# First loads of an attention and token-mixing kernel in another order: half of k by a hardware queue, p by the casting queue, and a new step list

## The chip, the cores and the metric

The kernel runs on one core of a Trainium2 chip. The metric is the device time of one execution in microseconds, median of the runs. A core has five engines, each with an instruction stream of its own that runs in order: TensorE (PE, with its weight loads shown as PEld), VectorE (DVE), ScalarE (ACT), GpSimd (POOL) and SyncE (SP). They wait for each other by semaphores. Transfers go over 16 DMA engines and are issued from SP, ACT or POOL. In this kernel a transfer issued by POOL also casts (float32 in memory, bfloat16 in the buffer); the profile lists POOL's queue as q0, software_dynamic. Transfers issued by SP (q1) and ACT (q10) are hardware_dynamic, and copy without a cast.

## The reference

There are 8 batches of 8 heads, with 576 positions of 64 elements, and 32 packing queries `p` for each head. Attention is applied twice, then a token-mixing layer.

```python
def sm_attn(qq, kk, vv):
    s = scale * np.matmul(qq, kk.transpose(0, 1, 3, 2))
    a = np.exp(s - np.max(s, axis=-1, keepdims=True))
    a = a / (np.sum(a, axis=-1, keepdims=True) + 1e-09)
    return np.matmul(a, vv)
p_packed = sm_attn(p, k, v)                # 32 rows for each head
x = sm_attn(q, p_packed, p_packed)         # then heads side by side: (8, 576, 512)
wq, wk = x @ w_q, x @ w_k                  # 512 -> 64
W_tok = scale * np.einsum('bsd,btd->bst', wq, wk)
mixed = np.einsum('bst,btd->bsd', W_tok, x)
out = np.maximum(mixed, 0.0) @ w_out       # 512 x 512
```

Inputs and output are float32. The output has 9.4 MB, as have q, k and v each.

## The kernel before

The whole program is one string, `ORDER`, at the head of the file. Each item is a step, with the batch and part after dots, the engine after `@` (A is ACT, V is DVE, P is POOL, S is SP), and the banks of the PSUM after `=`. The loop at the end of the kernel goes through the string and issues each step. As every engine runs its own stream in order, the string fixes the order on each engine, and the order of the transfers on each queue; between engines only the data's dependences count. Nothing is left to a scheduler.

The steps of one batch b, in the order of the data:

- `LD.k`, `LD.v` (two transfers), `LD.q` bring in the batch on POOL's casting queue (L156 to L181). There are four buffers each. In batch 0, k and q come in two halves (`LD.h0`, `LD.g0` for k, `LD.r0`, `LD.q0` for q).
- `KT` and `QV` transpose k and q in blocks on DVE (L236, the helper of all such transposes).
- `S1` (L281, TensorE) multiplies p with k; `X1` (L292, ACT) takes the exponential; `TE` (DVE) transposes it; `PV` (L314) multiplies with v and, by a column of ones in v's buffer, sums up; `RC`, `PP` (DVE) divide and mask, `PT` transposes. The result is p_packed.
- `QK` (L335) multiplies p_packed with the small weights w_q and w_k, `QKE` copies it out, `QD` doubles a part of it on POOL.
- `S2` (L372) multiplies q with p_packed in chunks of rows; `X2` (L377, ACT), `RS` (L393), `RR` (L398, DVE) are the softmax's exponential, sum and reciprocal; `AM` (L404, mostly POOL) multiplies; `AT` (L413, L418) transposes the result on TensorE and `AE` copies it out.
- `WKQ` (L440, L445), `WE`, `GM` (L466), `GE`, `Y` (L476), `YE`, `MX` (L491), `MR` (L497), `RL`, `RLR`, `RLF` (L502, L504) are the token mixing with its relu; instead of the 576 x 576 matrix `W_tok` the kernel goes by a small one of 64 columns (`GM`, `Y`), which gives the same product.
- `OT`, `OH` (L539, L576) multiply with w_out, whose load is `LD.O`; `OE`, `OEF`, `OEH` copy out of the PSUM on ACT or DVE (L127, L131); `ST`, `STF`, `STH` store.

Batches overlap: the steps of three or four of them are interleaved by hand in the string. Stores on SP stand behind `HOLD.v7`, a tiny transfer that waits for the last v.

`WARM.n` issues float32 matmuls of n x 128 columns on zeros (L614), with no use for the result: they are fill on TensorE where the string expects it to wait, and run in its stream in order like any other step. `WARM.n.128` issues them 128 columns at a time.

The start of before: p comes in two halves by the hardware queues (`LD.N0` on ACT, `LD.N1` on SP, L160) as float32 into `p32`; `NC` casts them (DVE and ACT), `PX` transposes them into `pT`. The small weights follow on the same queues (`LD.W0`, `LD.W1`, L163) into `w32`; `WC` casts them on POOL. POOL's queue starts with k of batch 0 (`LD.h0`, `LD.g0`), then v, q, and k of batch 1.

All buffers of this start lie in the six output buffers `T["o"]`, which are not yet in use.

Of the kernel before, what the change touches and what calls it, by code (L numbers as in the profile page):

```python
# [647 lines left out]
```

## Time and profile before

| | |
|---|---|
| median of three runs | 104.16 us (104.09 to 104.93) |
| the profiled execution | 104.06 us |
| its span, first to last instruction | 102.2 us |
| TensorE (PE) busy | 92.8 us, 91% |
| DVE busy | 73.5 us |
| ACT busy | 65.1 us |
| POOL busy | 53.3 us |
| granted TensorE clock | 1.0 of full speed |
| transfers | 25.13 MB, casting queue 17.04 MB |

The page's second part shows the span in 40 slices of 2.55 us; a digit is a busy share in tenths. A row of instructions has the start, the duration, the engine, the line of the kernel, the operation, what it writes and reads, and a count if several stand together; in brackets stands how long the engine idled before it and what ended that. A row of a transfer's issue has its size and the time from the issue to the landing. A "landing" is when the data may be used.

### The profile page before, as it was taken

How to read it: one execution, taken by the hardware profiler on the slowest of the kernel's cores; microseconds unless marked ns; L12 is line 12 of the kernel's file. 1: busy time of each engine (PE TensorE's matmuls, PEld its weight loads, DVE VectorE, ACT ScalarE, POOL GpSimd, SP SyncE). 2: the span in 40 equal slices, each digit the busy share in tenths (PEclk: the TensorE clock that was granted, in tenths of full speed). 3: DMA queues.
4: the chain of work that ended last, by engine and by line, in shares of the span. 5: the costliest groups of instructions: out<-in, count | busy, mean ns of one | idle time of the engine just before them, and what ended most of it. 6: DMA issues, size and time to landing. Idle time of an engine off the chain costs nothing.

```text
span 102.2 us, 3594 instructions
## 1 busy us (share of the span) xinstructions
PE 92.8 (91%) x1536; PEld 54.6 (53%) x1536; DVE 73.5 (72%) x140; ACT 65.1 (64%) x111; POOL 53.3 (52%) x83
## 2 busy tenths in 40 slices
PE   5997999998599999999998899989999999999940
PEld 3895445555275633755636556643757564743420
DVE  4273396858978579888697979599999979349510
ACT  1320315198654767849977979887989897726440
POOL 5982877974039929724459483649715009300000
PEclk9999999999999999999999999999999999999999
DMA  1999999999999999999999999999999999997894
GB/s 25 257 233 208 213 211 215 204 213 208 207 208 209 212 208 212 214 208 208 213 208 208 214 211 206 214 210 211 249 249 391 410 418 408 417 389 281 330 368 153
DMA packets 13567, 25.13 MB, mean 246 GB/s; under 512 B 1072, under 2 KB 6448, under 8 KB 13552
## 3 DMA queue, kind: packets, MB, share of 16 engines
q0 software_dynamic: 9936, 17.04, 84.6%
q1 hardware_dynamic: 3056, 7.34, 18.7%
q10 hardware_dynamic: 560, 0.52, 1.9%
q8 instruction: 12, 0.20, 0.7%
q14 instruction: 3, 0.02, 0.1%
HBM read 30.15 MB, written 9.44 MB: 387 GB/s over the span
## 4 chain that ended last, share of the span: by engine, by line
PE 50%; DMA 21%; DVE 8%; POOL 7%; ACT 7%; issue 3%; SPq 1%; POOLq 0%; DVEq 0%; ACTq 0%
PE ps L539 26%; DMA q_sb<-in_q_dram 13%; DMA o<-in_moe_w_q_dram 8%; PE ps L372 4%; POOL a L404 4%; PE ps L314 3%; ACT e1T L292 3%; PE ps L418 3%; PE ps L445 3%; DVE rs L393 2%; PE ps L440 2%; PE ps L466 2%; PE ps L281 2%; ACT e L377 1%; DVE qT L236 1%
## 5 line engine op out<-in xcount | busy, mean ns | idle before, releaser
L539 PE MATMUL ps<-wout,relu 128*128 128x512 bf16 x124 | 30.6, 380 | 0.0
L404 POOL TENSOR_TENSOR a<-e,rr 128x256 bf16<-128x256 f32 (+2 forms) x18 | 19.5, 1098 | 16.9 <-DVE rr L398 6.4
L614 PE MATMUL ps<-o 128*128 128x128 f32 (+3 forms) x76 | 19.3, 398 | 1.2 <-DVE o L134 1.2
L539 PEld LDWEIGHTS <-relu 128*128 128x128 bf16 x124 | 10.7, 98 | 11.7 <-issue 1.1
L127 ACT ACTIVATE o<-ps 128x1024 f32<-128x1024 f32 (+2 forms) x13 | 11.4, 878 | 5.4 <-PE ps L539 5.2
L614 PEld LDWEIGHTS ps<-o 128*128 128x128 f32 x76 | 11.2, 206 | 5.3 <-issue 3.6
L502 ACT ACTIVATE relu<-ps 128x1024 bf16<-128x1024 f32 (+1 forms) x14 | 12.9, 967 | 1.1 <-PE ps L491 1.1
L292 ACT ACTIVATE e1T<-ps 128x576 bf16<-128x576 f32 x16 | 9.8, 655 | 5.3 <-PE ps L281 4.7
L377 ACT ACTIVATE e<-ps 128x256 f32<-128x256 f32 (+2 forms) x19 | 11.2, 622 | 2.8 <-PE ps L372 2.6
L393 DVE TENSOR_REDUCE rs<-e 128x16 f32<-128x512 f32 (+2 forms) x13 | 10.9, 841 | 2.3 <-ACT e L377 2.2
L236 DVE STREAM_TRANSPOSE kT<-k_sb 128x1152 uint32<-128x1152 uint32 (+1 forms) x9 | 11.0, 1226 | 2.0 <-DMA k_sb<-in_k_dram 2.0
L172 POOL DMA_DIRECT2D v_sb<-in_v_dram x16 | 10.0, 629 | 4.6 <-DMA v_sb<-in_v_dram 1.4
L236 DVE STREAM_TRANSPOSE qT<-q_sb 128x1152 uint32<-128x1152 uint32 (+1 forms) x10 | 11.0, 1112 | 0.4 <-DMA q_sb<-in_q_dram 0.2
L131 DVE COPY o<-ps 128x1024 f32<-128x1024 f32 (+2 forms) x7 | 6.6, 958 | 5.0 <-PE ps L539 2.7
L236 DVE STREAM_TRANSPOSE e<-e1T 128x288 uint32<-128x288 uint32 x16 | 7.4, 469 | 2.5 <-ACT e1T L292 2.0
L127 ACT ACTIVATE aT<-ps 128x128 bf16<-128x128 f32 (+2 forms) x11 | 5.0, 465 | 5.7 <-PE ps L418 3.3
L314 PE MATMUL ps<-v_sb,e 64*64 64x192 bf16 x288 | 7.7, 245 | 0.8 <-DVE e L236 0.5
L127 ACT ACTIVATE wkq<-ps 128x448 bf16<-128x448 f32 (+1 forms) x10 | 7.2, 729 | 1.8 <-PE ps L445 1.7
L314 PEld LDWEIGHTS <-e 64*64 64x64 bf16 x288 | 6.0, 107 | 2.7 <-DVE e L236 2.0
L372 PEld LDWEIGHTS <-qT 64*128 64x128 bf16 x320 | 5.4, 94 | 2.8 <-DVE qT L236 1.8
L372 PE MATMUL ps<-ppT,qT 64*128 64x64 bf16 x320 | 6.6, 190 | 0.3 <-DVE qT L236 0.2
L445 PE MATMUL ps<-aT,pqk 128*128 128x256 bf16 (+1 forms) x48 | 6.8, 246 | 0.0
(70 smaller groups left out, 131.7 us busy)
## 6 DMA issues: line engine op xcount, KB each, us to landing
v_sb<-in_v_dram POOLq DMA_DIRECT2D x16, 288.0 KB, 14.3
out_dram<-o SPq DMA_DIRECT2D x9, 512.0 KB, 8.6
k_sb<-in_k_dram POOLq DMA_DIRECT2D x7, 576.0 KB, 13.8
q_sb<-in_q_dram POOLq DMA_DIRECT2D x6, 576.0 KB, 13.5
out_dram<-o POOLq DMA_DIRECT2D x4, 512.0 KB, 9.4
out_dram<-o SPq DMA_DIRECT2D x5, 256.0 KB, 2.6
q_sb<-in_q_dram POOLq DMA_DIRECT2D x4, 288.0 KB, 10.5
out_dram<-orem SPq DMA_DIRECT2D x3, 256.0 KB, 7.7
```

Of the source, the lines that this page charges most:

```text
L127: nc.scalar.activation(o, i, COPY)
L172: nc.gpsimd.dma_start(v_bufs[b % NL][halves(i), 0:7:2], src)
L236: nc.vector.transpose(o, i)
L292: nc.scalar.activation(e1T[:, x], T["s1", b][x].rearrange("a c m -> a m c"), EXP, scale=scale)
L314: nc.tensor.matmul(T["pv", b][halves(cc), i], lhsT, rhs, start=n == 0, stop=n == R - 1, skip_group_check=True)
L372: nc.tensor.matmul(ps[:, y, t - t0, i], lhsT, rhs, start=e == 0, stop=e == 1)
L377: nc.scalar.activation(e2[:, t0:t1].rearrange("a t (i y n) -> a y (t i) n", i=2, y=2), T["s2", b, c].rearrange("a y t i n -> a y (t i) n") ...
L393: nc.vector.tensor_reduce(rs[:, t0 * H:t1 * H], src, axis=AX, op=ADD)
L404: e.tensor_tensor(a2[:, t0:t1].rearrange("a t i (u l) -> a (t i u) l", l=L), e2v(b, c), T["rr", b][:, t0 * H:t1 * H].to_broadcast((P, (t1 ...
L502: nc.scalar.activation(o, i, RELU)
L539: nc.tensor.matmul(ps, lhsT, wout[:, j, :], start=j == 0, stop=j == NJ - 1)
L614: nc.tensor.matmul(bank(int(bk), [w]), warm[:, 0:P], rhs, start=True, stop=True)
```

## The change

Four things change.

- `LD.h0` on the casting queue becomes `LD.H`, the first transfer on SP: the first half of k of batch 0 comes as float32 into `h32` (in output buffer 0). A new step `HC` casts it on ACT. The small weights, both now on SP, stand behind it; their buffer `w32` moves to output buffer 5.
- `LD.N0` and `LD.N1` go to the head of POOL's casting queue and write bfloat16 into `pbf` directly; the step `NC` and the buffer `p32` go. `LD.g0`, v, and q follow.
- On POOL, `LD.k1` stands behind `SET.aff`, `SET.mask`, `SET.v2` and `SET.v3`, and the casts of the small weights behind `LD.k1`. `LD.v2`, `LD.q2`, `LD.O`, `LD.k3` come behind the `AM` steps of batch 0.
- The string is laid out anew, to its end. The steps are the same (but for those named and the fill), in another interleaving, with other PSUM banks, and for some 35 of them another engine (ACT and DVE swap copies; three stores swap POOL and SP).

```diff
 ORDER = """
-LD.N0@A LD.N1@S SET.warm@V SET.v0@V SET.aT0@V SET.aT1@V SET.aT2@V SET.idf@V LD.W0@A LD.W1@S SET.tab@A LD.h0
-LD.g0 LD.v0 LD.r0 LD.q0 LD.k1 NC.0@V PX.0@V NC.1@A PX.1@V SET.aff@P SET.idb@V SET.v3@P KT.0.0@V SET.mask@P
-WC.1@P WC.0@P LD.k2 SET.v1@P LD.v1 SET.v2@P KT.0.1@V WARM.4=0 WARM.22.128=0 S1.0=0,1,2,3 X1.0.1@A TE.0.1@V
-X1.0.0@A TE.0.0@V WARM.8=4 PV.0.0=4,5 PV.0.1 RC.0@V PP.0.0@V PP.0.1@V LD.q1 PT.0@V WARM.6=6 QK.0=6 QKE.0@A
-QV.0.0@V QV.0.1@V QD.0@P WARM.4=7 S2.0.2=2,3 X2.0.2@A RS.0.2@V RR.0.2@V S2.0.0=0,1 LD.v2 S2.0.1=4,5 X2.0.0@A
...
-TE.1.1@V MX.0.0=4,5 X1.2.0@A LD.O PV.1.0=0,1 TE.2.0@V PV.1.1 X1.2.1@A TE.2.1@V RC.1@V LD.k3 PP.1.0@V PP.1.1@V
-PT.1@V MX.0.1=6,7 QV.1.2@V RLR.0@A QK.1=2 QKE.1@V RL.0.0@A WARM.3=3 S2.1.2=4,5 S2.1.0=0,1 RL.0.1@A X2.1.2@A
...
+LD.H@S LD.W0@S LD.W1@S SET.warm@V SET.v0@V SET.aT0@V SET.aT1@V SET.aT2@V SET.idf@V SET.tab@A LD.N0 LD.N1 LD.g0
+LD.v0 LD.r0 LD.q0 SET.aff@P HC@A KT.0.0@V PX.0@V PX.1@V KT.0.1@V SET.idb@V WARM.4=0 WARM.18.128=0 S1.0=0,1,2,3
+X1.0.0@A TE.0.0@V X1.0.1@A TE.0.1@V WARM.9=4 PV.0.0=4,5 SET.mask@P PV.0.1 RC.0@V SET.v2@P SET.v3@P PP.0.1@V
+PP.0.0@V PT.0@V LD.k1 WC.0@P WC.1@P QV.0.0@V WARM.6=6 QK.0=6 QKE.0@A LD.k2 QV.0.1@V WARM.6=7 S2.0.2=0,1
+X2.0.2@A RS.0.2@V SET.v1@P LD.v1 S2.0.1=2,3 S2.0.0=4,5 LD.q1 RR.0.2@V X2.0.1@A RS.0.1@V RR.0.1@V AM.0.2@P
...
+TE.2.1@V PV.1.0=2,3 PV.1.1 RC.1@V LD.v2 MR.0=0,1 RLR.0@A PP.1.0@V PP.1.1@V PT.1@V LD.q2 MX.0.1=4,5 RL.0.1@A
+LD.O MX.0.0=6,7 QK.1=0 QKE.1@A TE.2.0@V RL.0.0@A QV.1.2@V WARM.7=1 S2.1.2=2,3 LD.k3 X2.1.2@A LD.v3 RS.1.2@V
...
+S2.3.3=6,7 MX.2.0=2,3 TE.4.1@V X2.3.3@A OT.1.1 MX.2.1=0,1 RS.3.4@V RL.2.0@A PV.4.0=6,7 PV.4.1 LD.q5 RC.4@V
+RL.2.1@A OT.2.0=2,3 OT.2.1 RR.3.4@V AM.3.3@P OE.1.0@A PP.4.1@V PP.4.0@V OE.2.0@A PT.4@V QK.4=0 AT.3.3=1
...
+X1.6.0@A TE.6.0@V GM.4=6 X1.6.1@A OT.3.2=2,3 HA.5@P LD.r7 GE.4@A Y.4=4,5 QD.5@P OE.3.0@A LD.q7 TE.6.1@V
+PV.6.0=6,7 PV.6.1 RS.5.4@V YE.4@A RR.5.4@V AM.5.3@P MX.4.0=0,1 RC.6@V PP.6.0@V MR.4=4,5 RLR.4@A OT.3.3
...
+RLR.6@A MX.6.1=4,5 OT.5.1 RL.6.1@V AT.7.1=0 RL.6.0@A AM.7.0@P AT.7.0=1 AE.7.0@V OE.5.0@A AE.7.1@V ST.5.0
+OT.6.0=6,7 WKQ.7.0=4,5 WKQ.7.1 WKQ.7.2 WE.7.1@V ST.1.0 OT.6.2=2,3 OEF.6.2@V WE.7.0@A GM.7=1 GE.7@V ST.5.1
...
+OEF.7.0@A STF.7.1 STF.7.0 OEF.7.2@A STF.7.2 OH.7.0=3 OEH.7.0@A STH.7.0 OH.7.1=5 OEH.7.1@A STH.7.1@A
 """
...
-            (nc.sync if eng == "S" else nc.scalar).dma_start(p32[:, i * n:(i + 1) * n], src[i])
+            nc.gpsimd.dma_start(pbf[:, i * n:(i + 1) * n], src[i])
...
-        elif a == "h":
-            nc.gpsimd.dma_start(k_in[0][:, 0], pairs(k, 0)[:, 0])
+        elif a == "H":
+            nc.sync.dma_start(h32, pairs(k, 0)[:, 0])
...
-    p32 = T["o"][NO - 1].rearrange("a t n -> a (t n)")[:, 0:L * Dh // 2]
+    w32 = T["o"][NO - 1][:, 0].rearrange("a (x i n) -> a x i n", x=2, i=2)
+    h32 = T["o"][0].rearrange("a t n -> a (t n)")[:, 0:RQ * Dh]
...
-    w32 = T["o"][0][:, 0].rearrange("a (x i n) -> a x i n", x=2, i=2)
...
-    def NC(x, eng, bk):
-        n = L * Dh // 4
-        copy(eng, pbf[:, x * n:(x + 1) * n], p32[:, x * n:(x + 1) * n])
...
+    def HC(eng, bk):
+        copy(eng, k_in[0][:, 0], h32)
```

The fill of before, in order, is WARM.4, 22 (ahead of `S1.0`), 8 (ahead of `PV.0`), 6 (ahead of `QK.0`), 4 (ahead of `S2.0`), 6, 5, 3 (among the `AT.0`), 2, 3, 1, 5: 75 units of 128 columns. After it is 4, 18, 9, 6, 6, 6, 5, 3, 3, 1, 7 (between `QK.1` and `S2.1`), 4, 4, 1: 77 units. Behind `def NC` the lines of the changed file have numbers smaller by one.

More of the change, by code (lines that the diff above doesn't have):

```diff
@@ new lines @@
+AE.1.2@A AE.1.0@A PT.2@V WARM.1=4 QK.2=4 AT.1.1=5 WKQ.1.0=0,1 QKE.2@A WKQ.1.2 AE.1.1@A WKQ.1.1 WE.1.1@A
+QV.2.2@V S2.2.2=6,7 X2.2.2@A LD.q3 S2.2.3=2,3 WE.1.0@V GM.1=4 GE.1@V LD.v4 OT.0.2=0,1 Y.1=6,7 X2.2.3@A YE.1@A
+OT.0.0=4,5 MR.1=2,3 RLR.1@A MX.1.0=6,7 RL.1.0@A OT.0.3 OE.0.1@A RS.2.4@V RR.2.4@V OT.0.1 QD.2@P AM.2.2@P
+KT.3.2@V S1.3=2,3,6,7 X1.3.0@A OT.1.4=0 AT.2.2=1 OE.0.0@V X1.3.1@A TE.3.0@V TE.3.1@V AM.2.3@P AT.2.3=2
+MX.1.1=4,5 PV.3.0=6,7 AE.2.2@A PV.3.1 AE.2.3@V WKQ.2.0=2,3 WKQ.2.2 WKQ.2.1 OEF.1.4@A RC.3@V PP.3.0@V RL.1.1@A
@@ L589, in STF @@
         q.dma_start(orows(b)[:, :, t * D:(t + 1) * D], T["o", b][:, t])
-    steps = dict(NC=NC, WC=WC, PX=PX, PB=PB, KT=KT, S1=S1, X1=X1, TE=TE, PV=PV, RC=RC, PP=PP,
+    steps = dict(HC=HC, WC=WC, PX=PX, PB=PB, KT=KT, S1=S1, X1=X1, TE=TE, PV=PV, RC=RC, PP=PP,
                  PT=PT, QK=QK, QKE=QKE, QD=QD, QV=QV, S2=S2, X2=X2, HA=HA, RS=RS, RR=RR, AM=AM,
```

60 lines of the change are left out of this document (24 added, 36 removed).

## The prediction

> **What bounds the kernel now.** I read the page's slices first, then TensorE's busy time in three stretches, then the chain of work that ended last, then the landings of the loads beside the instructions that wait for them. The profiled execution took 104.06 us, its span is 102.2, so 1.86 us lie outside the span; the median of the runs is 104.16, 0.10 more. All sums below are made against 104.06.
>
> ```profile
> span 102.2 us, 3594 instructions
> PE   5997999998599999999998899989999999999940
> DMA  1999999999999999999999999999999999997894
> L614 PE MATMUL ps<-o 128*128 128x128 f32 (+3 forms) x76 | 19.3, 398 | 1.2 <-DVE o L134 1.2
> ```
>
> Two rows are nearly full: the DMA engines from the second slice on, and TensorE almost everywhere. But 19.3 us of TensorE's 92.8 are fill, the WARM matmuls of L614: 75 units of 128 columns, 0.257 us each.
>
> ```profile
> 8.68:35.30 26.62, 23.83 (x462) 13.95 (x463) 19.15 (x41) 13.44 (x28) 17.62 (x28) 1.00 1.15 210
> 35.30:98.40 63.10, 61.43 (x1035) 34.33 (x1031) 50.63 (x85) 49.17 (x81) 29.38 (x38) 1.00 1.08 272
> 98.40:102.20 3.80, 0.00 (x0) 0.00 (x0) 0.04 (x1) 0.38 (x1) 0.00 (x0) 1.00 0.63 225
> ```
>
> Each row is a stretch, its length, busy time (and instructions) of TensorE, weight loads, VectorE, ACT and POOL, the granted clock, DMA share and GB/s. From 35.3 us (first product with wout) to 98.4 TensorE idles 63.10 - 61.43 = 1.67 us and has no fill: this stretch is bound by its work, and a new layout can win at most these 1.67 us in it. Before 35.3 TensorE is busy too, but much of that is fill; there it waits for loads, for chains of small steps and, in order, for its own fill. The granted clock is 1.00 everywhere, across an idle of 0.54 us before S1.0 too.
>
> ```profile
> 1.50 7.96 DMA o<-in_moe_w_q_dram
> 9.58 0.54 POOL wqk L129 x2
> 13.64 13.18 DMA q_sb<-in_q_dram
> 26.84 1.39 DVE qT L236
> 28.28 0.31 PE ps L372 x6
> 35.48 0.86 PE ps L539 x4
> ```
>
> The chain of work says the same: POOL waits until 9.5 for the small weights, which holds back its next loads; then q of batch 1 takes 13.18 us from issue to landing (26.82), its transpose starts at once, and S2.1 (28.28) leads by the softmax and the transposes to OT.0 at 35.48. So what counts before 35.3 is when loads land, and which steps are tied to them.
>
> ```profile
> 1.95 0.55 POOL L156 DMA_DIRECT2D k_sb<-in_k_dram  x1
> k_sb<-in_k_dram POOLq DMA_DIRECT2D x1, 288.0 KB, 6.6
> 8.62 0.78 DVE L236 STREAM_TRANSPOSE kT<-k_sb 128x576 uint32<-128x576 uint32 x1 [1.01 <-DMA k_sb<-in_k_dram]
> 9.45 0.47 PE L281 MATMUL ps<-kT,pT 32*32 32x288 bf16 x30 [0.54 <-DVE kT L236]
> 2.49 1.26 POOL L172 DMA_DIRECT2D v_sb<-in_v_dram  x2
> v_sb<-in_v_dram POOLq DMA_DIRECT2D x1, 288.0 KB, 8.6
> 11.78 0.94 PE L314 MATMUL ps<-v_sb,e 64*64 64x192 bf16 x36
> 14.48 1.13 PE L614 MATMUL ps<-o 128*128 128x512 f32 x2
> 15.54 0.78 PE L372 MATMUL ps<-ppT,qT 64*128 64x64 bf16 x40
> ```
>
> The second half of k lands at 1.95 + 6.6 = 8.55 and its transpose waited for it; S1.0 follows at 9.45. The second of the two v loads, issued half-way through the pair at 3.12, lands at 3.12 + 8.6 = 11.7, and PV.0 starts at 11.78. So the start is tied to the queue of loads.
>
> **The change, part by part.** (a) The loads. Bytes read are the same before and after, in another order and by other queues.
>
> ```profile
> o<-in_p_dram ACTq DMA_DIRECT2D x1, 256.0 KB, 3.7
> o<-in_moe_w_q_dram SPq DMA_DIRECT2D x1, 128.0 KB, 8.0
> q10 hardware_dynamic: 36, 0.07, 94.7%
> q1 hardware_dynamic: 13, 0.03, 34.0%
> q0 software_dynamic: 15, 0.03, 45.0%
> q10 hardware_dynamic: 118, 0.06, 43.8%
> q1 hardware_dynamic: 22, 0.01, 10.3%
> ```
>
> The first three queue rows (packets, MB, share) are the first packets of each queue: ACT's at 2.2 to 2.6 us, SP's at 3.0 to 3.4, the casting queue's at 3.8 to 4.2. The last two are weights, at 5.5 to 6.0 and at 8.5 to 9.0, their end. SP's p was issued at 0.74 as ACT's was; I take its 0.8 us delay for its standing behind ACT's. H now stands alone on SP, so it should move from 2.2. Its 590 KB take 1.45 us at the stores' 410 GB/s and 2.3 us at 257 GB/s (page, second slice); I take 1.6, since the casting queue is silent until 3.8. ACT's p had its last packets at about 3.6 and landed at 0.74 + 3.7 = 4.44, so a landing takes some 0.85 us: H lands at 4.7 (bounds 4.5 to 6.2, the latter with SP's old start).
>
> Casting queue: before, two halves of k (590 KB written) passed from 3.8 to 7.7; at the steady 210 GB/s they need 2.8, so 1.1 us were lost to p's rest (some 0.14 MB) and the weights (0.26 MB). Now p (262 KB written) and half of k (295 KB) need 2.65; only the weights disturb, 1.1 x 0.26/0.40 = 0.7. The half of k lands at 3.8 + 2.65 + 0.7 + 0.9 = 8.05, 0.5 us sooner. Bounds: nothing lost to the weights, 7.35; H with SP's old start, half of it still to move at 3.8, 0.9 later, 8.95. As the queue is served in order and never empties, v, q and k1 to wout shift alike: -0.5, ends -1.2 and +0.4.
>
> POOL's issues: k1 now stands behind the affine select, the mask and two memsets of v (0.32 + 0.18 + 0.78 + 0.61 + 0.61, the last two kinds by the rows below), so at about 8.1 instead of 5.02; q0 still moves until about 13.5, so this is hidden. The weights' casts come after k1 instead of ahead of it; k2, v1, q1 behind them as before. v2, q2 and wout go behind AM.0 (to about 20.3 instead of 15.5): q1's packets run until 25.9, so hidden; cover 4 us.
>
> ```profile
> 6.05 0.61 POOL L205 MEMSET v_sb<- 128x576 uint32 x1
> 6.80 0.78 POOL L212 MEMSET mask<- 32x64 bf16 x4
> 5.61 0.63 ACT L127 ACTIVATE o<-o 128x512 bf16<-128x512 f32 x1 [2.05 <-DMA o<-in_p_dram]
> 6.27 0.64 DVE L236 STREAM_TRANSPOSE pT<-o 128x256 uint32<-128x256 uint32 x1 [0.67 <-ACT o L127]
> ```
>
> (b) Casts. The two casts of p go (0.46 DVE, 0.63 ACT); HC, 128x1152 on ACT, is new: at most 2.25 x 0.63 = 1.4, I take 1.2. VectorE: H 4.7 + 1.2, KT.0.0 0.73, PX 2 x 0.64 gives 7.9, before the half of k lands. Ready, no cost.
>
> (c) S1.0 to S2.0. Transpose at 8.05, S1.0 at 8.9 (was 9.45). The fill ahead of it has 22 units instead of 26 and ends sooner; an idle of 1 to 2 us. Behind S1.0 (0.4) nine units instead of eight, 9 x 0.25 = 2.25: PV.0 at 11.55, though v lands at 11.2 (was 11.78: -0.2). From PV.0 to S2.0 it was 15.54 - 11.78 = 3.76 with ten units; now twelve, 4.26: S2.0 at 15.8 (+0.25), though q lands at 14.1. The fill gives the loads' gain away.
>
> (d) S2.0 to OT.0.
>
> ```profile
> 26.41 0.31 DVE L236 STREAM_TRANSPOSE ppT<-pp 128x128 uint32<-128x128 uint32 x1
> ```
>
> AM.0 on POOL keeps its length. On VectorE TE.2.0 (0.47) now stands between PT.1 and QV.1. PT.1 ended at 26.41 + 0.31 = 26.72; PV.1 loses MR.0 and MX.0.0 ahead of it but inherits the +0.25, so PT.1 ends near 26.5, QV.1 starts at 27.0, not at q1's landing of 26.3, and ends at 28.4. TensorE has seven units (1.75) behind QK.1 at 26.8: 28.55. S2.1 at 28.5 (+0.25). From there 7.2 us to OT.0 as before; nine units instead of six (+0.75) fill a wait of about 0.7. OT.0: +0.3, ends -0.5 (all fill fits) and +1.2 (loads late, below).
>
> (e) 35.3 to 98.4. The same matmuls. Its larger waits:
>
> ```profile
> 54.29 0.62 PE L418 MATMUL ps<-idb,a 128*128 128x128 bf16 x8 [0.44 <-POOL a L404]
> 57.05 0.48 PE L281 MATMUL ps<-kT,pT 32*32 32x288 bf16 x32 [0.32 <-DVE kT L236]
> 67.97 0.94 PE L314 MATMUL ps<-v_sb,e 64*64 64x192 bf16 x36 [0.47 <-DVE e L236]
> ```
>
> The last goes: OT.3.2 (0.86) now runs ahead of PV.6 while VectorE makes TE.6; next late would be AT.5.3, whose AM.5.3 ends with it. The first grows by 0.15, as RC.4 now stands ahead of RR.3.4; the second stays (AE.3.3, KT.5 as before). -0.3, ends -1.67 (all idle gone) and +1.2 (as many new waits of 0.3 to 0.5 as these three). The 30-odd evictions that swap between ACT and VectorE cost nothing there: ACT idles 14 us and VectorE 12 of 63; without that cover each costs its 0.3 to 1.0 us. Of the loads, v7 goes behind AM.4 on POOL (some 5 us later, to about 62; its packets follow k7's, which land at 71.5, so 8 us of cover), and the store of orem that stood ahead of r7 and q7 comes behind them: 0.6 us sooner for q of batch 7, which nothing waits for. The other stores that change between POOL and SP find the DMA engines full until 92 (slices), so their order alone changes.
>
> (f) The end.
>
> ```profile
> 98.39 0.38 ACT L127 ACTIVATE o<-ps 128x256 f32<-128x256 f32 x1 [0.28 <-PE ps L576]
> out_dram<-o ACTq DMA_DIRECT2D x1, 128.0 KB, 2.5
> ```
>
> Both last evictions are on ACT now, 0.07 later. ST.5.0 goes out with OE.5.0, sooner than its old place behind ST.6.0, so less is queued at the end: up to the 0.4 by which 2.5 exceeds SP's 2.1. Together -0.1, ends -0.3 and +0.1.
>
> Sum: 104.06 + 0.3 - 0.3 - 0.1 = 103.96, say 104.0 (104.1 on the median's scale).
>
> **The rivals.** Weights late (slower). W0 and W1 took their 512 packets from 4.2 to about 9.0 on two queues; on one queue behind H they take 4.8 us if the turns are no matter (landing 3.8 + 4.8 + 0.85 = 9.5), and 9.6 if one queue gets half the turns of two (14.3). WC.1 then ends 0.9 later. QK.0 needs it at 14.0 and S2.0 stands behind QK.0, so it decides from a landing of 13.1; at 14.3 it costs 1.2, giving 105.2, and up to 0.3 more as k2 then leaves POOL too late to follow k1 without a hole: 105.5. For it: SP's weights trickled, 22 packets in the half microsecond from 8.5, while the casting queue was full. Against: 118 of ACT's passed in the half microsecond from 5.5. The Trainium skill, "DMA: Bandwidth & Descriptors", section "Queues, rings and completion order", says that each DMA engine goes round its queues packet by packet; by that one hardware queue against the casting queue gets one turn in two where two had two in three, so the weights come later and p and k sooner. The trace has queues sharing, but not which turn each got.
>
> Loads late (slower, within 1%). H with SP's old start lands at 5.5, the half of k at 8.95; S1.0 at 9.8, PV.0 behind its nine units at 12.45, S2.0 at 16.7, OT.0 +1.2: 104.06 + 1.2 - 0.4 = 104.9. For it: SP's q1 row. Against: the order in which the two queues began.
>
> Fill hidden, waits gone (faster). Loads at their early end of -1.2 and fill as short as the gaps give OT.0 -0.5; most of the 1.67 us of idle goes too, -1.0; end -0.2: 102.4. For it: fill fitted its gap in before (14.48 + 1.13 against S2.0 at 15.54). Against: QV.1 is held by VectorE.
>
> New waits in (e) (slower): three more like those shown, +1.2, 105.5. Among them ST.1.0, now on SP behind ST.5.0, whose landing OEF.7.1 needs near 95.5; issued near 89.5, it has 6 us. A store issued at 89.05 took 5.7.
>
> ```profile
> out_dram<-o SPq DMA_DIRECT2D x1, 256.0 KB, 5.7
> ```
>
> **How the numbers follow.** Two kernels this alike can be told apart from about 1%, 1.04 us: faster is under 103.1, slower over 105.2. Forecast 0.50, centre 104.0, its own range 103.4 to 104.7. Weights late 0.10. Loads late 0.13. Fill hidden 0.15. New waits 0.12. Faster: 0.15 and a little of the forecast's edge, 0.17. Slower: most of weights late and new waits, 0.20. Within 1%: 0.63. To leave out no more than 2 in 10, the range goes from 102.8, short of the fastest case, to 105.3, past the late loads and short of the two slowest.
>
> **What would show it.** Right: SP's first packets at 2.2 and H landed by 4.9; half of k near 8.05; S1.0 near 8.9, but S2.0 near 15.8 and OT.0 near 35.6; PV.6 without a wait; idle after OT.0 near 1.4. Wrong: S2.0 sooner than 15.3, or QK.0 waiting for a cast on POOL; wout's first product before 35.0 or after 36.2; idle after it over 2.5, or under 0.7.

## The result and the profile after

| | before | after |
|---|---|---|
| median of five runs on one chip | 104.09 us (103.97 to 104.93) | 105.75 us (105.23 to 105.95) |
| ratio to before, 95% interval | | 1.0133 [1.0102, 1.0164] |
| the profiled execution | 104.06 us | 105.95 us |
| its span | 102.2 us | 104.2 us |

The changed kernel is slower by 1.3%, more than the forecast of 104.0 and beyond its range (to 105.3). Executions that took over 1.5% longer than the fastest of their kernel are left out of every ratio here (e8 and e15 have too few others for one), and where a profile below is of such a one (e3, e4, e15), only the stretches named in the text are read from it.

From the page of after: the span, the slices of TensorE, granted clock, DMA and GB/s, and the fill.

```profile
span 104.2 us, 3569 instructions
PE   5995999999799999999988898999999999999910
PEclk9999999999999999999999999999999999999995
DMA  3999999999999999999999999999999999499981
GB/s 74 285 176 203 213 211 212 205 213 208 208 208 212 210 212 209 212 205 212 212 206 212 197 204 209 213 208 213 211 360 409 412 417 409 164 374 396 366 326 54
L613 PE MATMUL ps<-o 128*128 128x128 f32 (+3 forms) x76 | 22.3, 437 | 1.2 <-DVE o L134 1.2
```

Two things differ from before. Fill is 22.3 us instead of 19.3. And the DMA row, which was full up to its 36th slice before, has a hole near the end: slice 35 (88.5 to 91.2 us), at 164 GB/s between 409 and 374.

The units of fill listed for before add up to 69, not to the 75 named with the list; after's 77 are thus eight more, four fewer ahead of S1.0 and twelve more behind it. The four fewer do not shorten the fill ahead of S1.0 (26 units of before, then 22 of after):

```profile
1.19 7.49 PE L614 MATMUL ps<-o 128*128 128x512 f32 x46 [1.19 <-DVE o L134]
1.19 7.47 PE L613 MATMUL ps<-o 128*128 128x512 f32 x38 [1.19 <-DVE o L134]
```

The first units run at half the speed of the later ones, and for how long differs by the execution: from 3.0 us on each half microsecond has 4 or 5 fill matmuls up to 4.0 in before and up to 6.0 in after, and 6 or 7 behind that. (The column of the granted clock reads 1.00 there all the same.)

After by three stretches (length; busy time and instructions of TensorE, weight loads, VectorE, ACT, POOL; clock, DMA share, GB/s), cut at the first product with wout and at the last matmul:

```profile
8.59:36.56 27.97, 25.67 (x472) 15.16 (x471) 19.19 (x42) 13.63 (x28) 17.11 (x27) 1.00 1.15 209
36.56:99.44 62.88, 60.34 (x1019) 34.33 (x1030) 48.79 (x84) 49.63 (x81) 28.87 (x37) 1.00 1.07 269
99.44:104.17 4.73, 0.00 (x0) 0.00 (x0) 0.00 (x0) 0.42 (x2) 0.00 (x0) 0.73 0.49 174
```

and before, cut at the end of its last matmul as well (98.36; its end row shown with the prediction begins at 98.40 and stops short of the span's end):

```profile
35.32:98.36 63.04, 61.41 (x1034) 34.31 (x1030) 50.59 (x85) 49.14 (x80) 29.36 (x38) 1.00 1.08 272
98.36:102.25 3.88, 0.00 (x0) 0.00 (x0) 0.08 (x1) 0.38 (x1) 0.00 (x0) 1.00 0.63 226
```

The middle stretch is about as long as before (62.88 against 63.04), so the 1.9 us by which the span grew lie at its two ends: the first product with wout (OT.0) comes at 36.56 instead of 35.32 (1.24), and from the last matmul to the end it takes 4.73 instead of 3.88 (0.85); 0.16 comes back between. (The middle row lists 1019 matmuls where before has 1034, and TensorE's busy time is short by those; the same layout with all its records is shown under e5.)

The start of after, from its timeline (start, length, engine, line, operation; in brackets the idle before it and what ended that):

```profile
4.34 1.16 ACT L127 ACTIVATE k_sb<-o 128x1152 bf16<-128x1152 f32 x1 [2.11 <-DMA o<-in_k_dram]
9.24 0.78 DVE L236 STREAM_TRANSPOSE kT<-k_sb 128x576 uint32<-128x576 uint32 x1 [0.71 <-DMA k_sb<-in_k_dram]
10.07 0.48 PE L280 MATMUL ps<-kT,pT 32*32 32x288 bf16 x30 [1.18 <-DVE kT L236]
12.62 0.94 PE L313 MATMUL ps<-v_sb,e 64*64 64x192 bf16 x36
15.31 1.56 PE L613 MATMUL ps<-o 128*128 128x512 f32 x4
16.80 0.78 PE L371 MATMUL ps<-ppT,qT 64*128 64x64 bf16 x40
36.56 1.03 PE L538 MATMUL ps<-wout,relu 128*128 128x512 bf16 x3
69.62 0.91 PE L313 MATMUL ps<-v_sb,e 64*64 64x192 bf16 x36
```

H is in by 4.34 and its cast takes 1.16, but the half of k on the casting queue lands at 9.2, not 8.05: S1.0 10.07, PV.0 12.62, S2.0 16.80, all without a wait behind S1.0. (The last row is PV.6: its wait of 0.47 is gone.) The chain of work that ended last (start, us, what) has changed its nature:

```profile
2.53 6.68 DMA k_sb<-in_k_dram
9.24 0.79 DVE kT L236
10.55 2.13 PE ps L613 x6
...
13.55 1.49 PE ps L613 x4
...
15.38 1.49 PE ps L613 x4
```

Before, the chain went by POOL's wait for the weights and q of batch 1. Now it goes by the half of k to S1.0 and then by TensorE's own fill (L613): whoever stands behind the fill waits for it.

The end, from the timelines of SP's queue and of ACT, and the issues from 96 us on (KB each, median us to landing):

```profile
83.74 1.18 SPq L557 DMA_DIRECT2D out_dram<-orem  x1
90.12 2.03 SPq L559 DMA_DIRECT2D out_dram<-o  x3
```

```profile
89.07 1.03 ACT L127 ACTIVATE o<-ps 128x1024 f32<-128x1024 f32 x1
```

```profile
out_dram<-o SPq DMA_DIRECT2D x3, 256.0 KB, 3.5
out_dram<-o ACTq DMA_DIRECT2D x1, 128.0 KB, 3.3
```

SP issues nothing from 84.9 to 90.1. ST.5.0 stands first in its stream there and waits for OE.5.0, which ends at 90.10; ST.1.0, whose data were ready long before, stands behind it. The DMA queues run nearly dry for a slice (2.6 us), and the last stores then take 3.3 to 3.5 us, the one of ACT 0.8 more than its 2.5 before.

### The profile page after: what moved, and what is told of

The parts are those of the page before. It is cut to its first block, busy times and chain, and to the rows that moved or that the text cites. A ratio compares the mean times of both kernels' runs of the same rounds, so it can differ in the third digit from the quotient of the medians.

```text
span 104.2 us, 3569 instructions
## 1 busy us (share of the span) xinstructions
PE 93.4 (90%) x1521; PEld 55.7 (54%) x1536; DVE 71.2 (68%) x138; ACT 66.3 (64%) x112; POOL 53.3 (51%) x83
## 4 chain that ended last, share of the span: by engine, by line
PE 68%; DVE 7%; DMA 6%; ACT 6%; POOL 5%; issue 3%; DVEq 0%; POOLq 0%; ACTq 0%
PE ps L538 25%; PE ps L613 13%; DMA k_sb<-in_k_dram 6%; PE ps L313 5%; PE ps L371 5%; POOL a L403 4%; PE ps L417 3%; PE ps L444 3%; PE ps L280 3%; PE ps L439 3%; PE ps L465 2%; DVE kT L236 2%; ACT o L127 2%; PE ps L334 2%; PE ps L475 2%
## 5 line engine op out<-in xcount | busy, mean ns | idle before, releaser
L538 PE MATMUL ps<-wout,relu 128*128 128x512 bf16 x112 | 29.9, 380 | 1.0 <-ACT relu L501 0.3
L613 PE MATMUL ps<-o 128*128 128x128 f32 (+3 forms) x76 | 22.3, 437 | 1.2 <-DVE o L134 1.2
L127 ACT ACTIVATE o<-ps 128x1024 f32<-128x1024 f32 (+2 forms) x17 | 14.8, 876 | 5.2 <-PE ps L538 5.2
L613 PEld LDWEIGHTS ps<-o 128*128 128x128 f32 x76 | 12.5, 222 | 6.2 <-issue 4.6
L127 ACT ACTIVATE wkq<-ps 128x448 bf16<-128x448 f32 (+1 forms) x8 | 5.7, 733 | 2.6 <-PE ps L444 1.5
L439 PE MATMUL ps<-pqk,aT 128*128 128x64 bf16 x80 | 5.9, 194 | 0.4 <-ACT aT L127 0.2
L127 ACT ACTIVATE aT<-ps 128x128 bf16<-128x128 f32 (+1 forms) x8 | 3.3, 407 | 4.6 <-PE ps L417 3.1
```

Source lines behind the costliest of these rows:

```text
L127: nc.scalar.activation(o, i, COPY)
L538: nc.tensor.matmul(ps, lhsT, wout[:, j, :], start=j == 0, stop=j == NJ - 1)
L613: nc.tensor.matmul(bank(int(bk), [w]), warm[:, 0:P], rhs, start=True, stop=True)
```

## The experiments

Each kernel is a small edit of before, of after or of another experiment; ratios are to before on the same chip. Medians are over all runs. Two theories stand against each other: the loads (the half of k 0.6 us later instead of 0.5 sooner) or the layout of the steps (the fill ahead of S2.0, the order of the stores).

**e1, the loads alone**: before with the new first loads; its list of steps is otherwise untouched.

```
-LD.N0@A LD.N1@S ... LD.W0@A LD.W1@S SET.tab@A LD.h0 LD.g0 ... LD.k1 NC.0@V PX.0@V NC.1@A PX.1@V
+LD.H@S LD.W0@S LD.W1@S ... SET.tab@A LD.N0 LD.N1 LD.g0 ... LD.k1 HC@A PX.0@V PX.1@V
```

> The step order of before with the loads of after. If p's slow pass over the casting queue delays the start and the new layout enlarges it, S1.0 starts near 10.0 as in after (before 9.45), S2.0 near 16.2 (before 15.54, after 16.80), the first product with wout near 35.7 to 36.0 (before 35.32, after 36.56), no late end, and 104.3 to 104.7 us in all. If the loads alone cost it all: 105.4 or more, first product near 36.5.

Measured: 104.33 us, ratio 0.9969 [0.9949, 0.9989]. The half of k lands at 9.6, S1.0 is at 10.44, OT.0 at 36.06. The loads alone do not slow the kernel.

**e2, the layout alone**: after with the first loads of before.

```
-LD.H@S LD.W0@S LD.W1@S ... LD.N0 LD.N1 LD.g0 ... HC@A KT.0.0@V PX.0@V PX.1@V
+LD.N0@A LD.N1@S ... LD.W0@A LD.W1@S SET.tab@A LD.h0 LD.g0 ... NC.0@V PX.0@V NC.1@A PX.1@V KT.0.0@V
```

> The step order of after with the loads of before. If fill and the store order are the larger part: S1.0 at 9.5, S2.0 near 16.3, first product with wout near 36.0, an end 0.9 us longer than before's 3.8 from the last matmul, 105.2 to 105.6 us. If the loads cost it all: 104.0 to 104.4.

Measured: 105.88 us, ratio 1.0131 [1.009, 1.0173], all of the slowdown. S1.0 is at 9.59, near before's 9.45, but OT.0 at 36.08, and the end comes 4.90 behind the last matmul.

```profile
9.59 0.48 PE L281 MATMUL ps<-kT,pT 32*32 32x288 bf16 x30 [1.04 <-DVE kT L236]
14.84 1.56 PE L614 MATMUL ps<-o 128*128 128x512 f32 x4
16.33 0.78 PE L372 MATMUL ps<-ppT,qT 64*128 64x64 bf16 x40
```

From S1.0 to S2.0 it takes 6.74 us, in after 6.73, before 6.09: the layout's 0.65, whatever the loads do. Three more units of fill stand on that way, and they are all of it: from its fill to PV.0 before takes 1.93 us with eight units (9.85 to 11.78) and after 2.14 with nine (10.48 to 12.62), from its fill to S2.0 before 1.06 with four (14.48 to 15.54) and after 1.49 with six (15.31 to 16.80). That is 0.21 to 0.22 a unit.

**e3, after with ST.1.0 ahead of ST.5.0 on SP.**

```
-... AE.7.1@V ST.5.0
-... WE.7.1@V ST.1.0 OT.6.2=2,3
+... AE.7.1@V ST.1.0
+... WE.7.1@V ST.5.0 OT.6.2=2,3
```

> After with one store, ST.1.0, ahead of ST.5.0 on SP, so that the DMA engines have work while SP waits for ST.5.0's data. If the long end comes of SP standing still from 84 to 90 us: the time from the last matmul's end to the span's end falls from 4.8 to 4.0 to 4.3, 0.5 to 0.8 us less in all. If the end is only shifted with the rest: no difference (within 0.2).

Measured: 106.13 us, ratio 1.011 [1.0072, 1.0147], hardly better than after. In its profile the end does shrink, to 3.90 behind the last matmul, but the start is another:

```profile
10.94 0.70 PE L280 MATMUL ps<-kT,pT 32*32 32x288 bf16 x30 [2.92 <-DVE kT L236]
11.57 3.61 PE L613 MATMUL ps<-o 128*128 128x512 f32 x6
```

```profile
7.61:11.02 3.41, 0.49 (x20) 0.26 (x25) 1.53 (x3) 0.00 (x0) 3.11 (x7) 1.00 1.18 202
11.02:14.44 3.42, 3.42 (x34) 1.44 (x34) 0.96 (x2) 1.19 (x2) 1.77 (x3) 0.50 1.11 208
14.44:15.44 1.00, 1.00 (x20) 0.64 (x22) 0.00 (x0) 0.00 (x0) 0.00 (x0) 1.00 1.12 214
```

The half of k landed at 10.1 here, and the fill had ended at 7.8 instead of after's 8.7, as its half-speed part was over near 4.2 us and not 6.0. TensorE stood idle for 2.92 us, and the granted clock (the column behind POOL) fell to 0.50 at 11.02 and came back at 14.44, so that nine units of fill took 3.61 instead of 2.21. It was the first sign that the fill ahead of S1.0, four units fewer than before, does work: it keeps the clock up. This run alone doesn't decide on the stores.

**e4, after with less fill** ahead of PV.0, S2.0 and S2.1.

```
-WARM.9=4 PV.0.0=4,5 ... WARM.6=7 S2.0.2=0,1 ... WARM.7=1 S2.1.2=2,3
+WARM.7=4 PV.0.0=4,5 ... WARM.3=7 S2.0.2=0,1 ... WARM.4=1 S2.1.2=2,3
```

> After with eight units of fill less: 7 instead of 9 ahead of PV.0, 3 instead of 6 ahead of S2.0, 4 instead of 7 ahead of S2.1. If the start's delay is fill that overstays: S2.0 near 15.9 (after 16.80), S2.1 near 28.0 (after 29.43), first product with wout near 35.3 (after 36.56), 1.0 to 1.3 us less in all. If loads or the other engines set these places: S2.0 and the first product move by less than 0.3 and TensorE idles instead.

Measured: 105.54 us, ratio 1.0049 [1.0017, 1.0081]. Its profile, too, has an idle of 2.36 us before S1.0 and the clock at half behind it, so its S2.0 (17.92) tells nothing of the fill. The ratio favours the fill; the profile can't confirm it.

**e5, the layout alone with ST.1.0 ahead of ST.5.0**: e2 with the edit of e3.

> The new step order with the old loads (as in the run of the layout alone, 1.013 of before) and ST.1.0 ahead of ST.5.0 on SP. If SP's standing still makes the late end: time from the last matmul to the span's end 3.8 to 4.1 (4.94 in the layout alone), ratio to before 1.002 to 1.006. If the late end is only a shift of all stores: ratio 1.011 to 1.014 and an end of 4.7 or more.

Measured: 104.88 us, ratio 1.0039 [1.0009, 1.0069], against e2's 1.0131: 0.9 us of 104.5. S2.0 and OT.0 are where e2 has them (16.33, 36.09), and the end is 3.91 behind the last matmul instead of 4.90.

```profile
DMA  2999999999999999999999999999999999988974
```

```profile
36.09:98.96 62.87, 61.37 (x1034) 34.35 (x1030) 48.49 (x84) 49.62 (x81) 28.88 (x37) 1.00 1.08 272
```

```profile
out_dram<-o SPq DMA_DIRECT2D x3, 256.0 KB, 2.4
out_dram<-o ACTq DMA_DIRECT2D x1, 128.0 KB, 2.5
```

The hole in the DMA row is gone, and the last stores land in 2.4 and 2.5 us. That the order of two stores costs 0.9 to 1.0 us in this layout is shown: the four profiles with ST.1.0 first (e3, e5, e7, e10) end 3.90 or 3.91 behind the last matmul, the eight with ST.5.0 first (after, e2, e4, e6, e8, e9, e13, e14) 4.73 to 5.12. The profiles of the old layout alone would not do for this: they end 3.88 to 3.96 behind it in three cases (before, e1, e15), but 4.37 in e11 and 5.19 in e12, whose last stores take longer too; why is open. The second row is the middle stretch of this layout with nearly all records: TensorE idles 62.87 - 61.37 = 1.50 us in it.

**e6, after with 26 units ahead of S1.0** as before has (`WARM.18.128` to `WARM.22.128`).

> After with the old 26 units of fill ahead of S1.0 instead of 22. If runs with a half clock come from TensorE's idle ahead of S1.0: no stretch below a granted clock of 1.0, idle ahead of S1.0 under 2.5 us, runs within 0.8 us of each other, median 1.010 to 1.014 of before. If the half clock comes by chance: some runs 1.5 us above the others again.

Measured: 106.10 us, ratio 1.0142 [1.0069, 1.0215]. The half of k lands at 9.4, S1.0 is at 10.26 behind an idle of 1.25, OT.0 at 36.76. By itself it wins nothing that the ratio shows, nor does it lose; the four runs have mean clocks of 0.992 or more but lie 1.0 us apart, not within 0.8.

**e7, the three mends together**: after with 28 units ahead of S1.0, the fill of e4 and the stores of e3.

> After with all three mended: 28 units of fill ahead of S1.0, eight units less behind it (7, 3, 4 instead of 9, 6, 7), ST.1.0 ahead of ST.5.0. If fill, clock and store order make up the slowdown: S2.0 near 16.2, first product with wout near 35.6, an end of 3.8 to 4.1, ratio to before 0.996 to 1.003. If something else in the new layout costs the time: 1.007 or more.

Measured: 104.35 us, ratio 0.9979 [0.9944, 1.0013]. The slowdown is gone: S1.0 9.71, S2.0 15.61, OT.0 35.00, the end 3.90 behind the last matmul. The half of k landed early here, at 8.9.

```profile
9.71 0.51 PE L280 MATMUL ps<-kT,pT 32*32 32x288 bf16 x32
15.61 0.81 PE L371 MATMUL ps<-ppT,qT 64*128 64x64 bf16 x40
```

**e8, p back on a hardware queue** (ACT's, as float32 with the two casts of before), the half of k first on the casting queue, 26 units ahead of S1.0.

```
-SET.tab@A LD.N0 LD.N1 LD.g0 ... HC@A KT.0.0@V PX.0@V PX.1@V
+LD.N0@A LD.N1@A SET.tab@A LD.g0 ... HC@A KT.0.0@V NC.0@V PX.0@V NC.1@A PX.1@V
```

> After with 26 units of fill ahead of S1.0 and p on ACT's hardware queue as float32 with its two casts, half of k still first on SP, so that the other half of k leads the casting queue. If p's pass over the casting queue is slow in itself: the second half of k lands at 7.3 to 8.4 (9.2 to 10.1 with p ahead of it), p by 7.2, S1.0 at 8.3 to 9.3. If the casting queue only starts slowly or the weights' small packets hold it: the half of k lands at 8.8 or later.

Measured: 109.06 us, median of four (107.08, 108.9, 109.22, 109.33). The profiled one (107.08) has the half of k at 8.8, though it leads its queue, as the second expectation has it (8.8 or later); p's second half lands at 9.0, and S1.0 is at 10.95, behind p. The second weights land at 10.1, against 8.1 in after. So p is slow on the hardware queue as well when H moves beside it. Why the other three runs took 109 us is open: their mean clocks of 0.982 and 0.983, against 0.988, speak for a stretch at half clock, but no profile shows it.

**e9, p's loads from contiguous rows**: e6, in which the two loads of p read contiguous rows of k in p's place. 

```
-src = p.rearrange("b (i c) (z l) d -> i (c z) b (l d)", i=2, z=4)
+src = k[1].rearrange("h s d -> (h s d)")[0:2 * P * n].rearrange("(i a m) -> i a m", i=2, m=n)
```

> The kernel after with 26 units of fill ahead of S1.0, in which the two casting loads of p read as many bytes from contiguous rows of k (2 KB a partition in one run) in place of p's scattered rows, so that what is computed is not the reference's; everything else stands as in the run with 26 units. There the second of the two loads landed at 7.7 us and the half of k at 9.4. Theory 'scattered rows': p is slow on the casting queue because of where its rows lie; then the second load lands by 6.9 and the half of k by 8.6. Rival 'the queue's start and its neighbours': the first packets of the casting queue are slow whatever they read, since H and the weights stand beside them; then the second load lands within 0.3 of 7.7 and the half of k between 9.0 and 9.8. The time is expected at 105.0 to 106.0 by both, as the store order and the fill stay.

Measured: 106.38 us, ratio 1.0173 [1.0105, 1.0241]. The second load lands at 7.6 (e6: 7.8), the half of k at 9.0 (9.4). The first is as the rival has it, the second at the rival's edge and inside the spread of the other runs. Where p's rows lie is not the main cause.

**e10, the layout with old loads, mended stores and less fill**: e5 with the edit of e4.

> The new layout with the old loads and with ST.1.0 ahead of ST.5.0 (ratio 1.0039 in its run), now with the fill ahead of PV.0, S2.0 and S2.1 shortened from 9, 6 and 7 units to 7, 3 and 4 (the kernel before has 8, 4 and 3 there). Theory 'fill overstays': S2.0 falls from 16.33 to about 15.5 us and OT.0 from 36.09 to 35.3 to 35.5; ratio to before 0.995 to 1.000. Rival 'the small steps of the layout decide': S2.0 waits for the softmax and the transposes instead, stays over 16.0, OT.0 over 35.9; ratio 1.002 to 1.006.

Measured: 104.68 us, ratio 1.001 [0.9983, 1.0037]. The half of k landed at 9.7 in its profile, S1.0 at 10.55, so S2.0 at 16.42 misses the expected 15.5; the way itself is shorter, 5.87 us from S1.0 to S2.0 and 25.42 from S1.0 to OT.0, against 26.49 in e2. The ratio alone can't tell it from e5 (the intervals overlap).

**e11, the loads alone with less fill**: e1 with `WARM.8=4` to `WARM.6=4` and `WARM.4=7` to `WARM.2=7` ahead of PV.0 and S2.0.

> The old layout with the new loads (ratio 0.9969 in its run), with the fill ahead of PV.0 and S2.0 shortened from 8 and 4 units to 6 and 2. Theory 'fill overstays there too': S2.0 comes 0.4 to 0.9 us sooner than that run's 16.52 and OT.0 up to 0.5 sooner than its 36.06; ratio 0.992 to 0.996. Rival 'loads set it': S1.0 at 10.4 and the landings stay, PV.0 waits for its softmax or S2.1 for q of batch 1; OT.0 within 0.2 of 36.06, ratio 0.996 to 0.999.

Measured: 104.07 us, ratio 0.9953 [0.9928, 0.9977], the best version here, below before and after. But the fill is not shown to be why. From S1.0 to S2.0 it is 0.42 shorter than in e1, and from S1.0 to OT.0 it is 25.64 against 25.62: S2.1 then waits for the transpose of q, as it did before.

```profile
28.22 0.78 PE L371 MATMUL ps<-ppT,qT 64*128 64x64 bf16 x40 [0.19 <-DVE qT L236]
```

OT.0 is sooner than e1's because the half of k landed at 8.8 instead of 9.6. The rival, that the loads set it, holds in its mechanism; OT.0 (35.27) and the ratio lie outside the numbers it gave, since it took the landings to stay.

**e12, the idle by itself**: before with `WARM.22.128` cut to `WARM.10.128`, 14 units ahead of S1.0 instead of 26.

> The kernel before with 14 units of fill ahead of S1.0 instead of 26, and nothing else: TensorE stands idle some 3.5 us before S1.0 where it stood 0.54. Theory 'the clock falls after a long idle': the profile shows a granted clock near 0.5 for some 3 to 4 us from about 10 to 14 us, the fill behind S1.0 takes twice its 0.25 us a unit, S2.0 comes 1.5 to 2 us later than before's 15.5, and the time is 105.5 to 106.2 against 104.2 to 104.5. Rival 'the idle costs nothing': clock 1.0 throughout, S2.0 within 0.3 of 15.5, time within 0.3 of before.

Measured: 107.76 us, ratio 1.0281 [1.023, 1.0332], more than expected, by the expected mechanism.

```profile
5.78:9.19 3.41, 1.27 (x11) 0.96 (x10) 2.04 (x6) 0.63 (x1) 1.36 (x7) 1.00 1.13 226
9.19:12.61 3.42, 2.61 (x33) 1.15 (x33) 1.71 (x3) 1.19 (x2) 2.37 (x5) 0.50 1.18 209
12.61:16.02 3.41, 3.41 (x40) 1.63 (x38) 0.00 (x0) 0.00 (x0) 2.12 (x4) 0.50 1.12 212
16.02:17.00 0.98, 0.98 (x3) 0.50 (x4) 0.78 (x3) 0.00 (x0) 0.00 (x0) 1.00 1.13 214
```

The fill ends at 6.75; in the next 3.25 us TensorE is busy for 0.30, and S1.0 comes at 10.00. The clock falls at 9.19 and is back at 16.02: 6.83 us at half speed, in which eight units took 3.78 us. (The half of k landed at 9.1, 0.55 later than in before's profile; that much of the delay is not the clock's.) In e3 the half clock lasted from 11.02 to 14.44, in e4 from 11.57 to 14.98, 3.4 us each. The Trainium skill, "TensorE: Matmul & The Clock Gate", section "Part 1: The HAM clock gate", says that about 3.4 us without work halve the clock, and about as long with work restores it. The traces agree in the length, with one such length in e3 and e4 and two in e12. They do not ask for a stretch without any work: in the 3.41 us up to the fall TensorE was busy for 0.49 us in e3, 1.05 in e4 and 1.27 in e12. In e6 and e10, counted in the same lengths from the end of the half-speed fill, the emptiest stretch has 2.17 and 2.20 us of work (7.84 to 11.26, 9.48 to 12.89), and the clock stayed. So what counts is how an idle lies to these stretches, and not only how long it is.

**e13, the weights behind H's cast**: e6 with the weights issued by ACT behind HC (`HC@A LD.W0@A LD.W1@A`) instead of by SP behind H.

> The kernel after with 26 units of fill ahead of S1.0 (p's second load landed there at 7.7 us, the half of k at 9.4), with the two weight loads issued by ACT behind its cast of H, near 5.6, in place of SP's issues at 1.2 and 1.7. Theory 'the weights beside it': p passes alone, its second load lands by 7.1; the half of k then has the weights beside it from about 7.5 and lands between 8.5 and 9.0. Rival 'p's small packets': the second load lands at 7.4 to 7.8, the half of k at 9.2 or later, since the weights now only disturb it elsewhere. Time 105.0 to 106.3 by both, as store order and fill stay.

Measured: 106.73 us, ratio 1.0206 [1.0159, 1.0253]. p's second load lands at 7.0 (e6: 7.8), the half of k at 8.6 (9.4), as the first theory has it. The time is over the expected 106.3: QK.0 now waits 0.53 us for the weights, and k2 goes out at 15.2 instead of 9.2.

**e14, the weights far behind**: e6 with the weights issued by ACT behind its first exponential (`X1.0.0@A LD.W0@A LD.W1@A`).

> As the run before this one, but the weights are issued by ACT behind its first exponential, near 11 us, so that no hardware load stands beside p and the half of k once H has passed. Theory 'the weights beside it': p (262 KB) and the half of k (295 KB) pass at the steady 205 to 210 GB/s from 3.9 us, 2.7 us; the half of k lands at 7.4 to 8.1. Rival 'p's small packets': p takes 1.6 to 2.6 us of the queue whatever stands beside it, the half of k 1.4 to 1.7, and it lands at 8.4 to 9.0. The weights land near 14.5 and hold QK.0 and S2.0 up to 1 us, so the time is no measure here: 105 to 107.

Measured: 111.87 us, ratio 1.0697 [1.0642, 1.0753]. QK.0 waits 4.42 us for the cast of the weights, far more than the 1 us expected; POOL's later loads stand behind that cast. The half of k lands at 8.7, p's second load at 6.9. The queues in the same half microsecond, 4.5 to 5.0 (packets, MB, share), first after, then e14, and below it all packets of e14 from 7.8 to 8.2:

```profile
q0 software_dynamic: 52, 0.04, 56.1%
q1 hardware_dynamic: 102, 0.05, 40.4%
```

```profile
q0 software_dynamic: 70, 0.06, 104.1%
DMA packets 61, 0.07 MB, mean 179 GB/s; under 512 B 1, under 2 KB 59, under 8 KB 61
```

With the weights beside it, p has 56% of the DMA engines' time and moves 0.04 MB; alone it has all of it, and still moves only 0.06 MB in half a microsecond, 129 GB/s, not the 210 (0.105 MB) that was reckoned. The last row shows a second thing. The packets of the half of k are over 2 KB, those of p and v under it; of the 61 packets two are still k's, though v's have been passing since 6.75. So the loads of a queue do not pass in one file: the last packets of k pass more than a microsecond behind the first of v, and k lands behind them (8.7). Both theories hold a part: the weights some 0.7 us of the half's landing (9.4 to 8.7, two single executions out of a spread of over 1 us), and the pass of p and k by themselves the rest.

**e15, e11 with the weights behind H's cast.**

> The old layout with the new loads and the fill ahead of PV.0 and S2.0 shortened (ratio 0.9953 in its run, half of k at 8.8, S1.0 at 9.6), with the weights issued by ACT behind its cast of H. Theory 'the weights beside it': the half of k lands 0.4 to 0.8 sooner, S1.0 starts near 9.2, behind its fill; OT.0 0.1 to 0.5 sooner than 35.27; ratio 0.990 to 0.995. Rival 'p's small packets': no sooner landing, and the weights, now later, hold POOL's casts and k2 behind them: OT.0 at 35.3 to 35.8, ratio 0.995 to 1.000.

Measured: 109.33 us, median of six (107.42 to 110.7). The half of k lands at 8.0 and S1.0 is at 8.91, right behind its fill, the soonest of all. But the weights, issued at 4.41 and 4.89 beside the full casting queue, need 8.0 and 10.7 us:

```profile
o<-in_moe_w_q_dram ACTq DMA_DIRECT2D x1, 128.0 KB, 10.7
```

```profile
16.47 0.41 PE L334 MATMUL ps<-wqk,ppT 64*64 64x128 bf16 x8 [2.55 <-POOL wqk L129]
```

In after the same transfer, issued at 1.65, needs 6.4. QK.0 waits 2.55 us for its cast, k2 goes out at 16.4 instead of 8.7, and all that was won at the start is lost several times over.

## Why the prediction was wrong

Two steps of it failed, (a) and (f). Against the forecast sum after's OT.0 came 0.94 us late (36.56 instead of 35.62), the middle stretch took 0.14 more and the end 0.95 more.

**Step (f), the end, forecast as -0.1, was +0.85.** It said that ST.5.0 "goes out with OE.5.0, sooner than its old place behind ST.6.0, so less is queued at the end". The first half is true. What was left out is that SP issues in order: with ST.5.0 ahead, ST.1.0 and ST.5.1 cannot go out before OE.5.0 ends at 90.10, the DMA queues run nearly dry for 2.6 us, and the bytes that should have moved then stand ahead of the last stores. e2 against e5 measure it by itself: 0.99 us in the profiles, 1.0131 against 1.0039 in the ratios. The rival "new waits" looked at this very pair of stores, but at who needs the landing of ST.1.0 (OEF.7.1; it landed at 90.80 + 4.3 = 95.1, and nothing waited), not at what stands behind the waiting store.

**Step (a), the half of k at 8.05, was 9.2**, beyond the bound of 8.95, and S1.0 came at 10.07 instead of 8.9. H came as predicted (by 4.34 against 4.7, so its start on SP was right), the casting queue started at 3.9 (3.8 forecast), and the weights were not late (landed at 4.7 and 8.1). The term that failed is the 2.65 us for p and the half of k "at the steady 210 GB/s". p moves 129 GB/s even with nothing beside it (e14, 4.5 to 5.0), at which its 0.26 MB alone take 2.0 us instead of 1.25; and the last packets lag. With no weights beside them the two loads take from 3.6 to 8.2 in e14, 4.6 us and not 2.65. The 0.85 us from the last packets to the landing was no fixed sum either: in e14 it is 0.55 (8.19 to 8.74). Later loads did not "shift alike": v came 0.4 later than before, k1 0.3 sooner.

The landings vary, and no single one may be read too closely. The half of k landed

| | us |
|---|---|
| old loads (before, e2, e5, e12, e10) | 8.6, 8.7, 8.7, 9.1, 9.7 |
| p ahead, weights on SP (e11, e7, e9, after, e6, e1, e4, e3) | 8.8, 8.9, 9.0, 9.2, 9.4, 9.6, 9.8, 10.1 |
| p ahead, weights later (e15, e13, e14) | 8.0, 8.6, 8.7 |

So the 0.7 us that (a) gave to the weights fits in size, and the gain of 0.5 over before is nowhere but in e15, where the weights were held back.

**Steps (c) and (d), the fill, held.** The fill does give the loads' gain away. The clean measure is the way from S1.0 to OT.0, free of when the half lands:

| S1.0 to OT.0, us | |
|---|---|
| before | 25.87 |
| e1, e11 (old layout, new loads) | 25.62, 25.64 |
| after, e2, e6, e9 (new layout) | 26.49, 26.49, 26.50, 26.50 |
| e10, e7 (new layout, less fill) | 25.42, 25.29 |

The forecast was 35.6 - 8.9 = 26.7. The new layout takes 0.62 more than before, the same to 0.01 us with old and new loads, early and late. With eight units less in three places (2, 3 and 3) the way becomes 1.1 to 1.2 shorter, and S2.1 waits for q again (0.35 and 0.18). What was off is the size of a unit: 19.3 us over 75 units gave 0.257, but there are 69, and the first of them run at half speed; on this way one more costs 0.21 to 0.22, and the three ahead of S2.0 cost 0.65 instead of the forecast's 0.8 (6.9 - 6.09). Nor did the fill ahead of S1.0 end sooner with four units fewer (8.66 against 8.68), as its half-speed part lasted longer. With S1.0 at 8.9 the sum would have held; S1.0 came 0.62 later than before instead of 0.55 sooner, and so OT.0 +1.24 (0.62 + 0.62) and not +0.3. That is the rival "loads late" almost to the number at the start (S1.0 9.8, S2.0 16.7, OT.0 +1.2), and with the end's 0.85 us on top.

How much of the 0.62 at S1.0 is the change's is less sure, as the table of landings overlaps. By e1 the new loads cost nothing on balance; the old layout is 0.4 us shorter behind OT.0 with them (62.65 and 62.63 in e1 and e11 against 63.04 and 63.02 in before and e12, from OT.0 to the last matmul); which wait that was, no row shows. In the ratios all of the slowdown is the layout's (e2 1.0131, after 1.0133): the order of the stores for 0.9 us of it, shown by e5; the rest fits the 0.62 of fill, which the profiles show and the ratios of e5 and e10 (1.0039 and 1.001, with intervals that overlap) do not decide.

**Right** were: (b), HC 1.16 against 1.2 and no cost; POOL's later issues hidden; and step (e). PV.6 runs without a wait, the waits of AT.3 and S1.5 stay (0.45 and 0.32), and TensorE idles 1.50 us there (e5) against the 1.4 forecast. None of the "new waits in (e)" came.

What no step had: the fill ahead of S1.0 guards the clock. An idle of "1 to 2 us" was forecast there at no cost. It was 1.18 in after, and the clock stayed at 1.00 until behind the last matmul; but the half's landing varies (8.8 to 10.1), and so does the end of 22 units of fill (7.8 in e3, 9.25 in e5), and where a late landing met an early end the idle was 2.4 to 2.9 and the clock fell (e3, e4). A stretch of 3.4 us at half clock takes 3.4 x 0.5 / 104 = 0.016 off the mean: of 46 runs with 22 units (after, e2 to e5, e10) 10 have a mean granted clock of 0.984 or less, of 40 with 26 or 28 units and the weights not late (e1, e6, e7, e9, e11, e13) 2, and none of the 61 of before beside e1, e5 and e10 is under 0.99. (Three of e8's four, with 26 units and p late, are at 0.982 or 0.983. A mean near 0.988, as after's, tells nothing of the start: the clock of 0.73 in the 4.73 us behind after's last matmul makes it.) For 14 units e12 shows the loss by itself; for 22 it is argued from these counts and the two profiles.

Open remain what makes the last packets of a load lag, and with it the landings vary by over a microsecond; and what made three of e8's four runs so slow.

## What to carry to other kernels

A store that is moved ahead in an in-order queue because its data come soon must be judged by what stands behind it: look for the idle of the issuing queue and for a hole in the DMA row, not only at who needs the landing. Fill on an in-order engine is a cost as soon as the work behind it is ready, so measure the way between two marks behind the last load (here 26.49 or 26.50 in every profile of one layout that kept its clock), and keep the fill in front of an uncertain load long enough for its late cases, since there an idle of some 2.5 us can cost the clock. Price a unit of fill from two places that differ by a unit, not from a total with slow ones in it. A queue's steady rate holds for its steady transfers; for the first ones, with small rows and neighbours, take the rate from the nearest rows of that stage, and look for the last packet rather than for the bulk.

## What the hardware showed unexpectedly

- The granted clock of TensorE changes at times that lie whole multiples of 3.41 us apart: it fell and came back at 11.02 and 14.44 (e3), 11.57 and 14.98 (e4), 9.19 and 16.02 (e12). It fell behind 3.41 us with 0.49, 1.05 and 1.27 us of work in them, stayed behind 2.17 and 2.20 (e6, e10), and did not come back behind 3.42 us with 2.61 of half-speed work (e12).
- TensorE's fill runs at half speed until 4 to 7 us into the program, by the execution (4.0 in before, 6.0 in after, 7.3 in e5), so that 22 units ended when 26 did (8.66 and 8.68).
- The packets of two loads on the casting queue pass beside each other, and a load lands with its last ones: in e14 v's pass from 6.75 on, k's until 8.2, and k lands at 8.7.
- The same 128 KB of weights take 6.4 us to land when issued at 1.65 us and 10.0 to 10.7 us when issued at 4.8 us, beside a casting queue that is full by then (after, e13, e15). The Trainium skill, "DMA: Bandwidth & Descriptors", section "Queues, rings and completion order", has each DMA engine go round its queues packet by packet; by that a transfer that meets the casting queue from start to end gets its turns one for one and its small packets carry little in each, and the trace agrees in direction.
- Casting loads of p, written in rows of 1 KB, move 129 GB/s with no other transfer beside them (e14, 4.5 to 5.0), where the casting queue moves about 210 later on.
